# Attention by bit patterns: two shifted copies summed by an accumulating DMA, two value passes a tile for three

## The chip, the cores and the metric

The kernel runs on one core of a Trainium2 chip. The metric is device time in microseconds (us): the median of three runs is 708.62 us (708.62 to 708.87). One more execution was recorded by the hardware profiler; its span, from the first to the last instruction, is 706.9 us. Engines are named as the profile names them: PE (TensorE) does matmuls, PEld its weight loads, DVE (VectorE) and ACT (ScalarE) read its results from PSUM, POOL (GpSimd) works on SBUF only, and SP (SyncE) issues DMAs. L1280 is line 1280 of the kernel before.

## The reference

```python
def reference(A_x, A_wq, A_wk, A_wv, A_wo, B_x, B_w1, B_w2):
    # S = 2048 rows, D = 640, 32 query heads of 20, one shared key and value head, F = 1728
    xn = layernorm(A_x)
    q = (xn @ A_wq) in 32 heads;  k = xn @ A_wk;  v = xn @ A_wv
    p = softmax(q k^T / sqrt(20))
    return A_x + (p v) @ A_wo + silu(xn @ B_w1) @ B_w2
```

Most of the work is the attention's exponentials: 32 heads times 2048 queries times 2048 keys.

## The kernel before

**Tiles.** Keys are cut into 16 tiles of 128 (`kt`), queries into four chunks of 512, heads into eight sets of four; a group `g` is one query chunk with one set of heads, 32 groups in all. An item is one head, one group and one key tile: a score matrix of 128 keys x 512 queries, which fills one of the eight PSUM banks. There are 32 x 16 x 4 = 2048 items. PE makes the scores of an item with one matmul (`s_mm`, L1005); the four heads of a set use four different 32-row parts of the array, so up to four such matmuls run side by side. The products with the values are collected over all 16 key tiles in bank 7 (`UB`): one *value pass* (`pv_mms`, L1125) is four matmuls of 512 columns, one for each head.

**Two ways to an exponential.** ACT computes it exactly, two or three items at a time (L1090), and its tile then needs one value pass. DVE makes an approximation instead: L1280 (`p1`) adds a bias to the scores, which come in units of 1/128 of a power of two, and writes them as 16-bit integers; those bits, read as bf16, are a crude exponential whose error repeats with the fraction. Four items (all heads of one `g`, `kt`) form a *batch* in a buffer `z` of 128 x 2048. Two more copies with the bits shifted by 43 and by 85 (`SHIFT`) are then made from it: the first by DVE (L1321, buffer `s1`), the second by POOL (L1316, buffer `s2`; `POOL_J`). The three copies are weighted by `C_J` and averaged, which removes most of the error. The weights are put into three scaled copies of the values (`v_all`), and the sum of the three is made by three value passes into bank 7.

**Buffers.** There are three buffers for `z`, and two more once the query weights in them have been used; two each for `s1` and `s2` (`NW`), and a third for each once the query and hidden-layer jobs have read a part of the normalized input (`xnT`). A `z` is free again when all value passes of its batch are done, an `s1` or `s2` when the pass that reads it is.

**Other work.** PE also makes the query projections (q), the hidden layer of the feed-forward part (h) and the outputs (out, y, fin), all with `col_mm` (L395). At the end of a group DVE copies bank 7 away (L1173), and the division by the softmax sum goes through a reciprocal (L780), small DMAs on SP (L777, L782, L785), a multiply on POOL (L789) and DMAs to the place where the output matmuls read (L802).

**What sets the order.** The program holds a list scheduler (`Sched` and the loop at the end of `build`). It models each engine with written-out costs and builds one fixed instruction list for each engine: at each step the engine that is earliest in the model takes its best ready operation. Engines run their lists in order and wait for each other by semaphores (`emit`); when something comes later on the chip than in the model, the order does not change. PE takes ACT's next scores first; scores for DVE are taken when a bank is free and DVE would run dry (`dve_items`), and key tiles that DVE does not claim (`claim`) go to ACT. So the share of DVE follows from the model. `PLAN` is a string with one letter for every 10 us of modelled time; each letter picks a small variation of the rules. Operations marked `port` (L1316, L1321, L789) are kept from overlapping between DVE and POOL in the model, and `calm` makes L1316 and L789 wait for the last L1321 placed before them.

The profiled execution has 157 batches, that is 628 items on DVE and 1420 on ACT, and 3304 matmuls in value passes: 1420 and 157 x 12.

Of the kernel before, what the change touches and what calls it, by code (L numbers as in the profile page):

```python
# [8 lines left out]
BF16 = mybir.dt.bfloat16  # L9
# [17 lines left out]
LOG2E = math.log2(math.e)  # L27
QSCALE = 128.0 * LOG2E / math.sqrt(DH)
ESCALE = math.log(2.0) / 128.0
SHIFT = (0, 43, 85)  # L30
C_J = (1.0, 0.78515625, 0.62109375)
C_K = 0.32331863
ZBIAS = 128.0 * 127.0 + 128.0 * math.log2(C_K)
NJ = len(SHIFT)

ABUFS = ((0, 1, 2), (3, 4))
UB = 7
# [29 lines left out]
LOOKP = 1.0  # L67
POOL_SHIFT = 1900.0
POOL_J = (2,)
SWITCH = 105.0  # L70
SPRIO = 0.5
PIECE = 10000.0
# [18 lines left out]
RULES = dict(a={}, b=dict(keep=0.0), c=dict(lagp=3), d=dict(lagp=5), e=dict(lagp=0), f=dict(patience=200.0), g=dict(dwant=0.0),  # L91
             h=dict(zcap=4), i=dict(zcap=3), j=dict(homes=0), k=dict(leadmax=-1.0, lead=-1.0), l=dict(lead=0.08, leadmax=0.1),
             m=dict(need=560.0), n=dict(hold=0.0), o=dict(stay=460.0), p=dict(open=1), q=dict(slack=400.0), r=dict(hungry=1000.0), s=dict(claim=9), t=dict(open=3), u=dict(claim=4), v=dict(want=2))
PLAN = "baauqaocarjonimairnmrfnfdqmoomfujapcnmocdndifrjnaajoadarpmnrodqaqqnmada"


def rule(n):
# [45 lines left out]
def t_act(n):  # L143
    return 50.0 + 0.8333 * n
# [135 lines left out]
def build(nc, A_x, A_wq, A_wk, A_wv, A_wo, B_x, B_w1, B_w2, out, stack):  # L280
# [31 lines left out]
    wo_sb = sb([P, DC, D], BF16)  # L312
    wv_sb = sb([P, DC, SLOT], BF16)
    kT_rep = sb([P, S], BF16)
    v_all = sb([P, NJ, KT, SLOT], BF16)
    qT = sb([P, NQ, QW], BF16)
    Ebuf = sb([P, NSLOT * QW], BF16)
    z_t = [sb([P, HG * QW], BF16) for _ in range(NZ)]
# [121 lines left out]
    def zeros(n, k=QW):  # L440
# [1 line left out]
        return bass.AP(zero_t, z.offset, [list(z.ap[0]), [0, n], [1, k]])  # L442

    vw = v_all[:, :, :, :].rearrange("p j t r -> p (j t r)").rearrange("p (n k) -> p n k", k=QW)
    vms = act(lambda a: a.activation(vw, zeros(NJ * KT * SLOT // QW), AF.Copy), t_act(NJ * KT * SLOT), pre=[zero_op],
              reads=[res("zero")], writes=[res("v")], prio=0.6)
    v1s = []
    for j, cj in enumerate(C_J):
# [696 lines left out]
    def pv_reg(op, g, flags):  # L1145
        def com(op):
            flags["first"] = not pv_started[g]
            pv_started[g] = True
            pv_left[g] -= 1
            att["value"] += 1.0 if op.name.startswith("PV" + str(g)) else 1.0 / NJ  # L1150
            flags["last"] = pv_left[g] == 0
            if pv_left[g] == 0:
                end_group(g, op)
        op.on_commit = com
        op.gate = lambda: att["pgroup"] == g
        pv_ops[g].append(op)
# [58 lines left out]
    def claim():  # L1215
        if z_slot() is None:
            return None
        g = att["sgroup"]
        left = len(unclaimed[g]) if g < NGR else 0
        if left < ru.claim and g < NGR - 1:  # L1220
            g += 1
        if g >= NGR or len(unclaimed[g]) == 0 or g not in q_op or not all(o.done for o in q_op[g]):
            return None
        if len(unclaimed[g]) < (ru.claim if g < NGR - 1 else max(ru.claim, 9)):
            return None
        ready = [kt for kt in unclaimed[g] if kt in kT_op and kT_op[kt].done and all(o.done for o in v_op[kt // 4])]
        if not ready:
            return None
        kt = ready[-1]
        unclaimed[g].remove(kt)  # L1230
        pv_left[g] += NJ - 1
        return (g, kt)

    ln_done = [False]
# [53 lines left out]
    def dve_advance(job):  # L1288
        st = job.batch
        st["left"].remove(job.head)  # L1290
        st["p1"].append(job.consumers[0])
        if st["left"]:
            return
        open_b.remove(st)
        g, kt, zi = st["g"], st["kt"], st["zi"]
        z = z_t[zi]
        zr = [res("z", zi, i) for i in range(HG)]
        N = HG * QW
        closed.append(st)
        z16 = z[:, :].bitcast(I16)  # L1300
        st["nth"] = len(closed)
        src = [([z[:, i * QW:(i + 1) * QW] for i in range(HG)], st["p1"], zr)]
        for j in range(1, NJ):
            qk = XQ[j - 1]
            if qk is not None and len(s_last[j - 1]) == NW[j - 1] and len(xq_read[qk]) == DC + FC and all(o.done for o in xq_read[qk]):
                s_last[j - 1].append(sc.order["pe"][-1])
            wi = min(range(len(s_last[j - 1])), key=lambda k: -1 if s_last[j - 1][k] is None or k == NW[j - 1] and isinstance(s_last[j - 1][k], Op) else s_last[j - 1][k]["nth"])
            old = s_last[j - 1][wi]
            s_last[j - 1][wi] = st
            lent = wi == NW[j - 1]  # L1310
            t = xnT[:, 0:HG, qk * QW:(qk + 1) * QW] if lent else s_t[j - 1][wi][:, :]
            zin = z16.rearrange("p (h q) -> p h q", h=HG) if lent else z16
            r = res("s", j, wi)
            args = dict(pre=st["p1"] + ([idb] + [norm_op[n] for n in range(NT)] if old is None else [old] if isinstance(old, Op) else [old["pv"][j]]), reads=zr, writes=[r], name=f"s{j}")
            if j in POOL_J:
                op = pool(lambda v, t=t, j=j, zin=zin: v.tensor_scalar(t.bitcast(I16), zin, float(SHIFT[j]), 1.0, ALU.add, ALU.mult),  # L1316
                          POOL_SHIFT, prio=0.3, **args)
                op.port = True
                op.gate = calm(op)
            else:  # L1320
                op = dve(lambda v, t=t, j=j, zin=zin: v.tensor_scalar_add(t.bitcast(I16), zin, float(SHIFT[j])), t_dve(N, 4),  # L1321
                         prio=SPRIO - 0.01 * j, **args)
                op.port = True
                op.on_commit = shifts.append
            src.append(([t[:, i, :] if lent else t[:, i * QW:(i + 1) * QW] for i in range(HG)], [op], [r]))
        st["sh"] = [pre[0] for _, pre, _ in src[1:]]
        st["pv"] = []
        for j, (t, pre, rd) in enumerate(src):
            flags = {}

            def f(pe, t=t, j=j, flags=flags):
                lst = [(v_all[:, j, kt, :], t[i], i) for i in range(HG)]
                return pv_mms(pe, g, lst, flags["first"], flags["last"])
            pv = Op("pe", f, 222.0, pre=pre + v_op[kt // 4], reads=rd + [res("vv", kt // 4, j)],
                    writes=[sc.banks[UB]], mode="p", prio=1.5, name=f"PVd{g}_{kt}")
            pv_reg(pv, g, flags)
            st["pv"].append(pv)
# [438 lines left out]
def emit(nc, sc, dma_sems, sem):  # L1776
# [8 lines left out]
    for e, ops in order.items():  # L1785
        for op in ops:
            for d in op.deps:
                if d.eng == "sp":
                    continue
                if d.eng == e and e == "pe":  # L1790
                    continue
                needed.add(d)
# [19 lines left out]
    while n_done < total:  # L1812
        moved = False
        for e in order:
            while ptr[e] < len(order[e]):
                op = order[e][ptr[e]]
                if any(d not in clock for d in op.deps if not (d.eng == e)):
                    break
                know = last[e]
                req = {}  # L1820
                for d in op.deps:
                    if d.eng == "sp":
                        k, v = ("d", d.dma_sem), dval[d]
                    else:
                        if d.eng == e and e == "pe":
                            continue
                        k, v = ("e", d.eng), val[d]
                    if know.get(k, 0) < v:
                        req.setdefault(k, (0, None))
                        if v > req[k][0]:  # L1830
                            req[k] = (v, d)
                items = sorted(req.items(), key=lambda kv: -kv[1][1].seq)
                for k, (v, d) in items:
                    if know.get(k, 0) >= v:
                        continue
                    s = dma_sems[k[1]][0] if k[0] == "d" else esem[k[1]]
                    prog[e].append(("w", s, v))
                    know[k] = v
                    for kk, vv in clock[d].items():
                        if know.get(kk, 0) < vv:  # L1840
                            know[kk] = vv
                if op.dma_sem is not None:
                    prog[e].append(("d", op.fn, dma_sems[op.dma_sem][0]))
                elif op in needed:
                    prog[e].append(("i", op.fn, esem[e]))
                else:
# [86 lines left out]
```

## Time and profile before

| what | value |
|---|---|
| median of three runs | 708.62 us |
| span of the profiled execution | 706.9 us |
| granted TensorE clock, mean | 0.999 |
| ACT: first exponentials to the end, busy | 100 to 680 us: 577.1 of 580 us |
| DVE busy, 50 to 680 us | 565.9 of 630 us |
| POOL busy, 100 to 680 us | 304.2 of 580 us |
| DMA engines' mean share, 100 to 680 us | 0.22 to 0.26 in windows of 100 us (0.25 in the last, of 80 us) |
| bytes moved by DMA in the span | 28.97 MB |

The rows are from the page's head and from a table of busy time by windows. An engine's busy time counts what its instructions took, without overlaps; the time of one instruction can overlap the next one's, so a mean times a count can exceed it. A PE that is busy is not a PE at its peak, since its matmuls are pipelined. "Idle before, releaser" is the time an engine stood still before a group of instructions, and what ended it.

### The profile page before, as it was taken

How to read it: one execution, taken by the hardware profiler on the slowest of the kernel's cores; microseconds unless marked ns; L12 is line 12 of the kernel's file. 1: busy time of each engine (PE TensorE's matmuls, PEld its weight loads, DVE VectorE, ACT ScalarE, POOL GpSimd, SP SyncE). 2: the span in 40 equal slices, each digit the busy share in tenths (PEclk: the TensorE clock that was granted, in tenths of full speed). 3: DMA queues.
4: the chain of work that ended last, by engine and by line, in shares of the span. 5: the costliest groups of instructions: out<-in, count | busy, mean ns of one | idle time of the engine just before them, and what ended most of it. 6: DMA issues, size and time to landing. Idle time of an engine off the chain costs nothing.

```text
span 706.9 us, 22620 instructions
## 1 busy us (share of the span) xinstructions
PE 687.3 (97%) x9900; PEld 232.5 (33%) x9903; DVE 614.8 (87%) x1057; ACT 687.4 (97%) x730; POOL 360.2 (51%) x233
## 2 busy tenths in 40 slices
PE   8999999999999999999999999999999999999997
PEld 5432222222223333322233333322222233333334
DVE  7789999998999978899988889899889998887972
ACT  6999999999999999999999999999999999999994
POOL 6625645555456545555445455455554656544441
PEclk9999999999999999999999999999999999999999
DMA  8642221122221122322012222222222022232201
GB/s 220 199 144 39 19 21 18 32 31 30 18 30 17 22 39 29 67 34 26 16 21 29 29 38 33 55 30 27 29 20 21 7 32 32 32 63 29 18 7 39
DMA packets 34242, 28.97 MB, mean 41 GB/s; under 512 B 15487, under 2 KB 29663, under 8 KB 34143
## 3 DMA queue, kind: packets, MB, share of 16 engines
q1 hardware_dynamic: 33854, 27.20, 24.9%
q8 instruction: 77, 1.26, 0.7%
q10 hardware_dynamic: 288, 0.33, 0.1%
q14 instruction: 23, 0.18, 0.1%
HBM read 11.09 MB, written 2.62 MB: 19 GB/s over the span
## 4 chain that ended last, share of the span: by engine, by line
ACT 59%; PE 36%; DVE 2%; DMA 1%; POOL 0%; issue 0%; SPq 0%; DVEq 0%; POOLq 0%
ACT sbt L1090 56%; PE psall L1005 12%; PE psall L395 11%; PE psall L1125 11%; ACT sbt L709 3%; DMA sbt<-in_A_x_dram 1%; DVE sbt L1280 1%; PE psall L558 0%; DMA sbt<-in_A_wk_dram 0%; PE psall L532 0%; DVE sbt L894 0%; PE psall L1586 0%; PE psall L926 0%; PE psall L944 0%; DVE sbt L544 0%
## 5 line engine op out<-in xcount | busy, mean ns | idle before, releaser
L1090 ACT ACTIVATE sbt<-psall 128x1024 bf16<-128x1024 f32 (+1 forms) x658 | 666.1, 1227 | 4.5 <-PE psall L1005 3.9
L1280 DVE TENSOR_SCALAR sbt<-psall 128x512 int16<-128x512 f32 x628 | 412.5, 685 | 56.8 <-PE psall L1005 51.8
L1316 POOL TENSOR_SCALAR sbt<-sbt 128x2048 int16<-128x2048 int16 x157 | 298.2, 1899 | 303.3 <-DVE sbt L1321 112.0
L1005 PE MATMUL psall<-sbt 32*128 32x512 bf16 x2048 | 268.6, 384 | 9.0 <-ACT sbt L1090 5.4
L1125 PE MATMUL psall<-sbt 128*32 128x512 bf16 x3304 | 261.7, 384 | 2.7 <-DVE sbt L1173 2.5
L395 PE MATMUL psall<-sbt 128*32 128x320 bf16 (+2 forms) x3904 | 231.8, 331 | 0.6 <-DVE sbt L1280 0.2
L1005 PEld LDWEIGHTS psall<-sbt 32*128 32x128 bf16 x2048 | 71.4, 91 | 252.5 <-ACT sbt L1090 181.2
L395 PEld LDWEIGHTS psall<-sbt 128*32 128x32 bf16 x3904 | 83.8, 95 | 84.0 <-issue 53.0
L1321 DVE TENSOR_SCALAR sbt<-sbt 128x2048 int16<-128x2048 int16 x157 | 109.6, 709 | 1.8
L1125 PEld LDWEIGHTS psall<-sbt 128*32 128x32 bf16 x3304 | 65.5, 94 | 115.8 <-issue 76.8
L789 POOL TENSOR_TENSOR sbt<-sbt 128x512 bf16<-128x512 f32 x30 | 38.3, 1275 | 17.5 <-DVE sbt L1321 13.5
L712 DVE SCALAR_TENSOR_TENSOR sbt<-sbt,psall 128x512 bf16<-128x512 bf16 x52 | 35.4, 681 | 5.0 <-ACT sbt L709 2.9
L709 ACT ACTIVATE sbt<-psall 128x512 bf16<-128x512 f32 x52 | 39.3, 755 | 0.0
L1173 DVE COPY sbt<-psall 128x512 f32<-128x512 f32 x31 | 21.2, 683 | 0.1
L1586 PE MATMUL psall<-sbt 128*32 128x256 bf16 (+1 forms) x312 | 19.3, 355 | 1.2 <-DVE sbt L424 1.2
L630 DVE TENSOR_SCALAR sbt<-psall 128x512 bf16<-128x512 f32 x20 | 13.7, 683 | 0.5 <-PE psall L395 0.3
L831 DVE SCALAR_TENSOR_TENSOR sbt<-psall,sbt 128x320 bf16<-128x320 f32 x24 | 11.6, 483 | 1.7 <-PE psall L395 1.5
L522 POOL TENSOR_SCALAR sbt<-sbt 128x640 bf16<-128x640 bf16 x12 | 10.5, 880 | 2.3 <-DVE sbt L514 2.2
L1586 PEld LDWEIGHTS psall<-sbt 128*32 128x32 bf16 x312 | 8.8, 112 | 6.7 <-issue 2.3
L509 POOL TENSOR_TENSOR sbt<-sbt 128x2 f32<-128x2 f32 x8 | 5.6, 695 | 6.3 <-DVE sbt L507 6.2
L500 DVE BATCH_NORM_STATS2 sbt<-sbt 128x6 f32<-128x320 bf16 x14 | 6.5, 473 | 2.1 <-DMA sbt<-in_A_x_dram 1.9
L846 DVE SCALAR_TENSOR_TENSOR sbt<-psall,sbt 128x320 f32<-128x320 f32 x8 | 3.9, 482 | 4.8 <-PE psall L395 4.8
(61 smaller groups left out, 98.8 us busy)
## 6 DMA issues: line engine op xcount, KB each, us to landing
sbt<-sbt SPq DMA_DIRECT2D x120, 64.0 KB, 3.8
sbt<-in_A_x_dram SPq DMA_DIRECT2D x28, 160.0 KB, 4.1
sbt<-sbt SPq DMA_DIRECT2D x213, 20.0 KB
out_dram<-sbt SPq DMA_DIRECT2D x14, 160.0 KB, 1.9
sbt<-in_B_w_dram SPq DMA_DIRECT2D x1, 2160.0 KB, 11.4
sbt<-in_B_w_dram SPq DMA_DIRECT2D x1, 2080.0 KB, 8.1
sbt<-sbt SPq DMA_DIRECT2D x75, 8.0 KB
sbt<-in_A_wq_dram SPq DMA_DIRECT2D x1, 800.0 KB, 7.5
```

The lines of the kernel that those rows point to most:

```text
L395: ins = pe.matmul(ps[j * SLOT:(j + 1) * SLOT, b * BANK + off:b * BANK + off + n], w[:, j * SLOT:(j + 1) * SLOT], x, start=start, stop=stop ...
L709: t = Op("act", lambda a: a.activation(t_buf[0:rows, ts, :], bk(job.bank, 0, QW, rows=rows), AF.Tanh, scale=0.5), t_act(512), 215, pre=[jo ...
L712: u = Op("dve", lambda v: v.scalar_tensor_tensor(out=hT[par][0:rows, fk, :], in0=t_buf[0:rows, ts, :], scalar=1.0, in1=bk(job.bank, 0, QW, ...
L789: nm = pool(lambda e: e.tensor_tensor(oU[:, us, :], U_sb[:, us, :], Rrep, ALU.mult), 1350.0 + MARGIN, pre=[uc] + lc + pack_op.get(divmod(g ...
L1005: return pe.matmul(bk(b), kT_rep[i * SLOT:(i + 1) * SLOT, kt * P:(kt + 1) * P], qT[i * SLOT:(i + 1) * SLOT, g % NQ, :], start=True, stop=T ...
L1090: return a.activation(Ebuf[:, es * QW:es * QW + w], ps[:, buf[0] * BANK:buf[0] * BANK + w], AF.Exp, scale=ESCALE)
L1125: ins = pe.matmul(ps[i * SLOT:(i + 1) * SLOT, UB * BANK:UB * BANK + QW], lhsT, rhs, start=(first and k < HG), stop=(last and k >= len(lst) ...
L1173: uc = Op("dve", lambda v: v.tensor_copy(U_sb[:, us, :], bk(UB)), t_dve(512), 140, pre=[pv] + up, reads=[sc.banks[UB]], writes=[res("U", u ...
L1280: p1 = Op("dve", lambda v: v.tensor_scalar(z16[:, i * QW:(i + 1) * QW], bk(job.bank), ZBIAS, 0.0, ALU.add, ALU.max), t_dve(QW), 140, pre=[ ...
L1316: op = pool(lambda v, t=t, j=j, zin=zin: v.tensor_scalar(t.bitcast(I16), zin, float(SHIFT[j]), 1.0, ALU.add, ALU.mult), POOL_SHIFT, prio=0 ...
L1321: op = dve(lambda v, t=t, j=j, zin=zin: v.tensor_scalar_add(t.bitcast(I16), zin, float(SHIFT[j])), t_dve(N, 4), prio=SPRIO - 0.01 * j, **args)
L1586: ins = pe.matmul(ps[i * SLOT:(i + 1) * SLOT, UB * BANK:UB * BANK + n], zero_t[:, 0:SLOT], zero_t[:, 0:n], start=fresh, stop=fresh, tile_p ...
```

## The change

There are three shifts as before, now 0, 41 and 81, and the two shifted copies get the same weight. They can then be added before PE sees them: once L1321 and L1316 have written `s1` and `s2` of a batch, POOL issues one DMA that adds `s2` (128 x 2048 bf16, 512 KB) onto `s1` in place. A batch has two value passes, of `z` and of the sum; `v_all` keeps two scaled copies of the values. `s2` is free when the sum has landed, `s1` when the second pass is done. The model charges the DMA 1.0 us on POOL and 4.0 us more until it has landed, and treats it as a `port` operation. All engines' orders are computed anew with the new costs, and `PLAN` is another string.

```diff
-SHIFT = (0, 43, 85)
-C_J = (1.0, 0.78515625, 0.62109375)
-C_K = 0.32331863
+SHIFT = (0, 41, 81)
+C_J = (1.0, 0.65625)
+C_K = 0.3387
 NJ = len(SHIFT)
+NV = len(C_J)
...
+SUM_OCC = 1000.0
+SUM_LAT = 4000.0
...
-PLAN = "baauqaocarjonimairnmrfnfdqmoomfujapcnmocdndifrjnaajoadarpmnrodqaqqnmada"
+PLAN = "aaaqarpjrqaaprnpkrmmfhtqroaandodrmaaqaqmaadmrmtpqopmhtrqtnnqakrapankt"
...
-    v_all = sb([P, NJ, KT, SLOT], BF16)
+    v_all = sb([P, NV, KT, SLOT], BF16)
...
-        pv_left[g] += NJ - 1
+        pv_left[g] += NV - 1
...
+        held = []
...
-            args = dict(pre=st["p1"] + (... else [old["pv"][j]]), reads=zr, writes=[r], name=f"s{j}")
+            args = dict(pre=st["p1"] + (... else [old["sum"]] if j == 2 else [old["pv"][1]]), reads=zr, writes=[r], name=f"s{j}")
...
+            held.append(t if lent else t.rearrange("p (h q) -> p h q", h=HG))
...
+        (t1, p1, r1), (_, p2, r2) = src[1:]
+        tot = dma(f"sum{s1_home}", lambda e, a=held[0], b=held[1]: e.dma_start(a, b, accum_op=ALU.add), 0, pre=p1 + p2, reads=r2, writes=r1, prio=0.25, eng="pool")
+        tot.occ, tot.lat, tot.port = SUM_OCC, SUM_LAT, True
+        st["sum"] = tot
         st["pv"] = []
-        for j, (t, pre, rd) in enumerate(src):
+        for j, (t, pre, rd) in enumerate((src[0], (t1, [tot], r1))):
...
-                if d.eng == "sp":
+                if d.dma_sem is not None:
```

More of the change, by code (lines that the diff above doesn't have):

```diff
@@ L444, in build @@
     vw = v_all[:, :, :, :].rearrange("p j t r -> p (j t r)").rearrange("p (n k) -> p n k", k=QW)
-    vms = act(lambda a: a.activation(vw, zeros(NJ * KT * SLOT // QW), AF.Copy), t_act(NJ * KT * SLOT), pre=[zero_op],
+    vms = act(lambda a: a.activation(vw, zeros(NV * KT * SLOT // QW), AF.Copy), t_act(NV * KT * SLOT), pre=[zero_op],
               reads=[res("zero")], writes=[res("v")], prio=0.6)
@@ L1149, in com @@
             pv_left[g] -= 1
-            att["value"] += 1.0 if op.name.startswith("PV" + str(g)) else 1.0 / NJ
+            att["value"] += 1.0 if op.name.startswith("PV" + str(g)) else 1.0 / NV
             flags["last"] = pv_left[g] == 0
@@ L1310, in dve_advance @@
             lent = wi == NW[j - 1]
+            s1_home = wi if j == 1 else s1_home
             t = xnT[:, 0:HG, qk * QW:(qk + 1) * QW] if lent else s_t[j - 1][wi][:, :]
@@ L1313, in dve_advance @@
             r = res("s", j, wi)
-            args = dict(pre=st["p1"] + ([idb] + [norm_op[n] for n in range(NT)] if old is None else [old] if isinstance(old, Op) else [old["pv"][j]]), reads=zr, writes=[r], name=f"s{j}")
+            args = dict(pre=st["p1"] + ([idb] + [norm_op[n] for n in range(NT)] if old is None else [old] if isinstance(old, Op) else [old["sum"]] if j == 2 else [old["pv"][1]]), reads=zr, writes=[r], name=f"s{j}")
             if j in POOL_J:
@@ L1821, in emit @@
                 for d in op.deps:
-                    if d.eng == "sp":
+                    if d.dma_sem is not None:
                         k, v = ("d", d.dma_sem), dval[d]
```

## The prediction

> **What bounds the kernel now.** I read the page's busy times first, then the chain that ended last, then the groups of instructions with their releasers, then DVE's busy time by windows.
>
> ```profile
> PE 687.3 (97%) x9900; PEld 232.5 (33%) x9903; DVE 614.8 (87%) x1057; ACT 687.4 (97%) x730; POOL 360.2 (51%) x233
> ...
> ACT 59%; PE 36%; DVE 2%; DMA 1%; POOL 0%; issue 0%; SPq 0%; DVEq 0%; POOLq 0%
> ```
>
> ACT and PE are both full, and the chain goes back and forth between them: there is no single bound. DVE has 92 us free, POOL half its time.
>
> ```profile
> L1090 ACT ACTIVATE sbt<-psall 128x1024 bf16<-128x1024 f32 (+1 forms) x658 | 666.1, 1227 | 4.5 <-PE psall L1005 3.9
> L1280 DVE TENSOR_SCALAR sbt<-psall 128x512 int16<-128x512 f32 x628 | 412.5, 685 | 56.8 <-PE psall L1005 51.8
> L1316 POOL TENSOR_SCALAR sbt<-sbt 128x2048 int16<-128x2048 int16 x157 | 298.2, 1899 | 303.3 <-DVE sbt L1321 112.0
> ...
> L1125 PE MATMUL psall<-sbt 128*32 128x512 bf16 x3304 | 261.7, 384 | 2.7 <-DVE sbt L1173 2.5
> ...
> L1321 DVE TENSOR_SCALAR sbt<-sbt 128x2048 int16<-128x2048 int16 x157 | 109.6, 709 | 1.8
> ```
>
> ACT is never short of scores (4.5 us idle before 658 exponentials). DVE is: 51.8 us of its idle time ends with a score matmul. So PE time saved helps ACT only by a detour: PE feeds DVE earlier, DVE claims more batches, and ACT has fewer items.
>
> ```profile
> 300.79 0.39 PE L395 MATMUL psall<-sbt 128*32 128x512 bf16 x4
> 301.12 0.45 PE L1005 MATMUL psall<-sbt 32*128 32x512 bf16 x3
> 301.50 0.61 PE L395 MATMUL psall<-sbt 128*32 128x512 bf16 x8
> 302.05 0.39 PE L1005 MATMUL psall<-sbt 32*128 32x512 bf16 x2
> 302.37 0.61 PE L395 MATMUL psall<-sbt 128*32 128x512 bf16 x8
> ```
>
> Four matmuls show 0.39 us and eight 0.61, so one more pass of four costs PE 0.22 us. From one score set to the next is 0.93 us, filled without a gap.
>
> ```profile
> 100.00:150.00 50.00, 47.26 (x78) 1.00 0.28 31
> ...
> 400.00:450.00 50.00, 42.00 (x67) 1.00 0.22 30
> 450.00:500.00 50.00, 47.55 (x80) 1.00 0.26 39
> ```
>
> These windows (length, DVE busy, instructions, clock, DMA share, GB/s) show where room is: 42.0 of 50 us where PE makes output matmuls, 47.6 elsewhere. From 50 to 680 us DVE is idle 630 - 565.9 = 64 us.
>
> **The change, part by part.**
>
> *The third pass goes.* 157 x 0.22 = 34.5 us of PE time. By itself that shortens nothing, as ACT stays full.
>
> *Batches move from ACT to DVE.* An item costs ACT 666.1/1420 = 0.469 us, a batch 1.88 us. A batch costs DVE 4 x 412.5/628 + 109.6/157 = 3.33 us. If n batches move, the span falls by 1.88n, and DVE's idle time falls by (3.33 + 1.88)n = 5.2n. What idle time is left? In its fullest window before DVE has 2.4 of 50 us idle (47.6 busy), which would be 30 us in 630 and n = 6.5; none left would be n = 12.3. The waits on scores occur in the full windows too, so I take half of 30: (64 - 15)/5.2 = 9.4 batches, 17.7 us. From both sides: 12 us (n = 6.5) to 23 us (n = 12.3). PE then has about 687 - 34.5 + 2 = 655 us of work in 689, and its cover is real: were PE still full, n would be 0.
>
> *POOL's new issue.* No DMA is issued by POOL before. The bounds are 0.1 us (its smallest memset row) and 1.9 us (its own pass over the same tile); SP's issues of copies inside SBUF take 0.59 us median (L785). I take 1.0, between the near row and the upper one. 166 x 1.0 on POOL's 360 gives about 535 of 689 us: not a bound, so nothing in the sum; at 1.9 it would be 690, full. The issue waits for L1321 and for POOL's own L1316; behind it in POOL's list stand the next L1316 and the multiply L789, and behind L789 SP waits at L802 (103.6 us already, in SP's own waits), with the query copies of L643 behind that. POOL's 303 us of idle time before L1316 hides this.
>
> *The sum's way.* Before, the last pass followed L1316; now it follows L1316, the issue and the landing. Landing times by row:
>
> ```profile
> sbt<-sbt SPq DMA_DIRECT2D x120, 64.0 KB, 3.8
> ...
> out_dram<-sbt SPq DMA_DIRECT2D x14, 160.0 KB, 1.9
> sbt<-in_B_w_dram SPq DMA_DIRECT2D x1, 2160.0 KB, 11.4
> sbt<-in_B_w_dram SPq DMA_DIRECT2D x1, 2080.0 KB, 8.1
> ...
> sbt<-in_B_w_dram SPq DMA_DIRECT2D x2, 80.0 KB, 2.3
> ```
>
> The bounds are 1.9 us (a third of the bytes) and 11.4 (four times). Between 80 KB at 2.3 and 2080 KB at 8.1 lie 2.9 us per 1000 KB. An addition must read both tiles, 1024 KB: 2.3 + 2.7 = 5.0 us. Started from the 64 KB row, a copy inside SBUF but out of a single row per head, it is 6.6. I take 5.0. The order allows 1.0 + 4.0 = 5.0, so PE has no wait in the sum; each microsecond beyond is priced with the rivals.
>
> The page "DMA: Bandwidth & Descriptors" of the Trainium skill (section "Anatomy of one DMA — SWDGE (gpsimd) path") fits 2.0 us plus the bytes at 436 GB/s for DMAs from GpSimd; as an estimate that is 3.2 us for 512 KB and 4.4 us with both tiles counted. By it the sum stays as it is, and the late landing below would be worth a chance of only 0.1.
>
> *Buffers.* `s1` is now held for 0.7 + 1.9 + 5.0 and some 2 us until PE gets to it, 9.6 us. A batch comes every 630/150 or so = 4.2 us: three buffers (12.6 us) suffice, two (8.4 us) do not, until the third is lent. I charge nothing: `z` and the later two thirds of the run are free of it, and until then it can cost at most one batch in eight, some 3 batches or 6 us; I keep that for the range.
>
> *Small things.* Four value scalings less on DVE (L590, 2.2/12 each) are 0.7 us of DVE, 0.3 us of span. Weights, shifts and the smaller `v_all` cost nothing: no instruction is added for them.
>
> **The sum.** 706.9 - 17.7 - 0.3 = 688.9 us of span; the runs' median lies 1.7 above the span before, so I add 1.7 and get 691 us.
>
> **The rivals.**
>
> *The sum lands late (slower).* Place: the second value pass in PE's fixed list. For it: 64 KB inside SBUF already take 3.8 us, and a row of one size scatters (11.4 and 8.1 for nearly the same bytes); DMA engines that stand at 0.2 now will carry some 87 MB more. Against it: L1316's passes hardly ever held PE before (2.1 us in nine waits, in the waits list), so the list leaves room. Price: from a batch's last score to its second pass is about 10 us, so a lateness of d is paid about 630/10 = 63 times, not once a batch, since PE's wait also delays what follows. The point from which it decides is 18/63 = 0.3 us beyond the room left. With 6.6 us instead of 5.0 and 1 us of room: 63 x 0.6 = 38 us, 691 + 38 = 729 us; without room 691 + 101 = 792.
>
> *The DMA engines fill up (slower).* The busiest window moves 277 GB/s at a share of 0.82. At that rate of 338 GB/s when full, 512 KB take 1.6 us and three times that (two reads, a write) 4.7; times 166 is 257 to 772 us, beside about 0.24 x 689 = 165. Only at the upper end does it bind: 772 + 165 = 937 us. From 3.2 us a sum on, it decides.
>
> *POOL and DVE block each other (a smaller gain).* One L1321 at 409.67 us took 2.03 us instead of 0.69 and ended just after three back-to-back L1316 passes: while POOL is at SBUF, this pass waits. A 1.0 us issue overlaps a 0.7 us L1321 at random with chance 1.7/4.2 = 0.4 and costs some 0.5 us then: 166 x 0.2 = 33 us of DVE, 33/5.2 x 1.88 = 12 us of span: 703 us. Against it: the order keeps the two apart, and only a few of 157 were longer than 0.9 us.
>
> The page "SBUF — State Buffer" of the Trainium skill (section "SBUF: two separate sides") speaks against this change: while VectorE runs in a two-port mode, GpSimd cannot write the descriptors of its DMAs, and the transfer stands still. The trace shows the block in the other direction only (the 2.03 us). By that rule a sum would be up to 0.7 us later, which belongs to the first rival.
>
> *The relief is not used (no change).* DVE's windows at 47.6 of 50 are nearly full, and the new order may give it no more batches; then ACT stays at 666 us and the time at 708.
>
> **How the numbers follow.** Forecast 691: 0.58, with its own range 681 to 700 (the bounds 12 and 23 us around it, and the buffers). Smaller gain, 703: 0.10. No change, 708: 0.06. Late sum, 729: 0.23. Full DMA engines: 0.03. Below 0.2%, 1.4 us, no change can be told from the measurement. Faster: 0.58 + 0.10 + 0.01 = 0.69; same 0.04; slower 0.23 + 0.03 + 0.01 = 0.27. The range goes from 679 to 729: the upper half of the late case and the full engines are left out, 0.15, and a little below.
>
> **What would show it.** Right: L1125 falls from 3304 to about 2700 matmuls, L1280 rises to about 665, ACT's L1090 falls to about 650 us and stays without idle time, DVE's idle before L1280 falls below 25 us, sums land within 5 us. Wrong: PE's weight loads for value passes wait for a DMA for more than a few us in all (late sum); L1321 means above 0.8 us (blocking); POOL above 90% busy; the DMA share near 1; L1280 still near 628 (relief not used).

## The result, and the profile after

The changed kernel takes 888.28 us (median of four runs, 883.88 to 891.53) against 708.75 us before (708.62 to 708.91): 1.253 times the time, 95% interval 1.2506 to 1.2553. The prediction was 691 us. The profiled execution has a span of 884.8 us, 177.9 us more than before. In the new listing the lines stand three lower in the first part and a few more behind the new code: L1093 is ACT's exponential, L1283 `p1`, L1321 POOL's shift, L1326 DVE's shift, L1334 the sum, L1128 the value pass, L1008 the scores, L792 the multiply of the normalization, L783 its reciprocal, L788 its last small DMAs.

From the page of the changed kernel: busy times, the clock granted to PE and the DMA engines' busy share in 40 slices (tenths), the DMA queues (packets, MB, share of 16 engines), the chain that ended last.

```profile
PE 745.4 (84%) x9704; PEld 236.0 (27%) x9707; DVE 632.8 (72%) x1048; ACT 705.2 (80%) x742; POOL 518.3 (59%) x387
...
PEclk9998998788889989999989798999788998799999
DMA  8676776767776868778569776777857777796773
...
q0 software_dynamic: 40128, 81.80, 53.4%
q1 hardware_dynamic: 33854, 27.20, 18.9%
...
DMA 34%; PE 23%; DVE 17%; POOL 12%; issue 8%; ACT 4%; SPq 3%; POOLq 0%; DVEq 0%
```

ACT and PE have fallen from 97% to 80% and 84%. The chain, 59% ACT before, is 34% DMA, and 33 of these points are transfers inside SBUF. The sums alone keep the sixteen DMA engines busy for 53.4% of the span; the clock, 0.999 in the mean before, is 0.906.

The groups of instructions (count, busy us, mean ns, idle before and what ended most of it):

```profile
L1093 ACT ACTIVATE sbt<-psall 128x1024 bf16<-128x1024 f32 (+1 forms) x670 | 676.8, 1111 | 156.3 <-PE psall L1008 154.3
L1283 DVE TENSOR_SCALAR sbt<-psall 128x512 int16<-128x512 f32 x624 | 410.0, 684 | 162.9 <-PE psall L1008 159.7
...
L1128 PE MATMUL psall<-sbt 128*32 128x512 bf16 x2672 | 243.8, 416 | 109.3 <-DMA sbt<-sbt 103.5
...
L1334 POOL DMA_DIRECT2D sbt<-sbt x156 | 162.1, 1084 | 131.6 <-DVE sbt L1326 104.8
L1326 DVE TENSOR_SCALAR sbt<-sbt 128x2048 int16<-128x2048 int16 x156 | 128.4, 837 | 7.7 <-PE psall L1128 7.2
...
L792 POOL TENSOR_TENSOR sbt<-sbt 128x512 bf16<-128x512 f32 x30 | 40.5, 1348 | 73.7 <-DMA sbt<-sbt 42.1
```

ACT's exponentials grew by 10.7 us and their idle time by 151.8 (4.5 before): together 162.5 of the 177.9. That idle time ends with a score matmul, so PE was late; and PE stood 103.5 us ahead of value passes for a DMA. DVE's items are 624, not more than the 628 before.

The DMA issues (count, KB, median us from issue to landing):

```profile
sbt<-sbt POOLq DMA_DIRECT2D x156, 512.0 KB, 6.4
sbt<-sbt SPq DMA_DIRECT2D x120, 64.0 KB, 5.4
```

The sum lands after 6.4 us (4.5 at least, 12.1 at most), where the order was made for 5.0. The small DMAs of the normalization, which the change does not touch, take 5.4 us in place of 3.8, and up to 9.7 (4.8 before). Part of that is their issue on SP, 1.08 us in the median for 0.59. Behind them stand POOL's L792 (42.1 us of waits in 12 places; 2.7 before) and DVE's L783 (19.3; none before). Behind the sums stand PE's value passes (the 103.5 us, in 58 places) and POOL's L1321, which may not write an `s2` that a sum still reads (35.3 us in 21 places). Followed back through the trace by the instruction that issued each transfer, the chain that ended last holds 248 us of sums in 31 pieces and 47 us of the normalization's small DMAs in nine.

One stall in PE's timeline (start us, us, instructions; in brackets the wait ahead of them):

```profile
399.93 0.40 PE L398 MATMUL psall<-sbt 128*32 128x512 bf16 x4
402.36 0.40 PE L1128 MATMUL psall<-sbt 128*32 128x512 bf16 x4 [2.04 <-DMA sbt<-sbt]
402.59 0.39 PE L398 MATMUL psall<-sbt 128*32 128x512 bf16 x4
403.73 0.40 PE L1128 MATMUL psall<-sbt 128*32 128x512 bf16 x4 [0.75 <-DVE sbt L1176]
...
404.88 1.90 PE L1128 MATMUL psall<-sbt 128*32 128x512 bf16 x16
```

And the busy times around it (stretch, its length, busy us of each engine with counts, clock, DMA share, GB/s):

```profile
400.00:404.00 4.00, 1.22 (x16) 0.25 (x16) 4.00 (x4) 2.31 (x3) 3.77 (x3) 1.00 0.48 92
404.00:406.00 2.00, 2.00 (x22) 0.66 (x22) 1.56 (x3) 1.43 (x2) 1.72 (x2) 0.56 0.87 126
406.00:408.00 2.00, 2.00 (x24) 0.57 (x16) 0.00 (x0) 0.93 (x2) 1.05 (x1) 0.59 1.18 172
```

PE waits 2.04 us for a sum and 0.75 us for the copy of bank 7, which stood on DVE behind two shifts that took 4.04 us together. Then its clock is 0.56 to 0.59 for 4 us: sixteen matmuls take 1.90 us, 0.43 a pass by their weight loads where a pass took 0.22. So this wait is paid again just after it. Over the run the missing clock is at most (1 - 0.906) x 884.8 = 83 us. PE is busy for 745.4 us; the same list of 9704 matmuls keeps it busy for 684.8 us at a clock of 1.0 (e2 below), 61 us less. How much of this lies on the path is not measured.

### The profile page after: what moved, and what is told of

Its sections match the earlier page's. It is cut to its first block, busy times and chain, and to the rows that moved or that the text cites. A ratio compares the mean times of both kernels' runs of the same rounds, so it can differ in the third digit from the quotient of the medians.

```text
span 884.8 us, 22460 instructions
## 1 busy us (share of the span) xinstructions
PE 745.4 (84%) x9704; PEld 236.0 (27%) x9707; DVE 632.8 (72%) x1048; ACT 705.2 (80%) x742; POOL 518.3 (59%) x387
## 3 DMA queue, kind: packets, MB, share of 16 engines
q0 software_dynamic: 40128, 81.80, 53.4%
## 4 chain that ended last, share of the span: by engine, by line
DMA 34%; PE 23%; DVE 17%; POOL 12%; issue 8%; ACT 4%; SPq 3%; POOLq 0%; DVEq 0%
DMA sbt<-sbt 33%; POOL sbt L1321 8%; PE psall L1008 8%; DVE sbt L1283 8%; PE psall L1128 7%; PE psall L398 7%; DVE sbt L1326 4%; ACT sbt L1093 4%; POOL sbt L1334 2%; PE psall L1596 1%; DVE sbt L1176 1%; SPq L805 1%; POOL sbt L792 1%; DVE sbt L715 1%; SPq L788 1%
## 5 line engine op out<-in xcount | busy, mean ns | idle before, releaser
L1093 ACT ACTIVATE sbt<-psall 128x1024 bf16<-128x1024 f32 (+1 forms) x670 | 676.8, 1111 | 156.3 <-PE psall L1008 154.3
L1283 DVE TENSOR_SCALAR sbt<-psall 128x512 int16<-128x512 f32 x624 | 410.0, 684 | 162.9 <-PE psall L1008 159.7
L1321 POOL TENSOR_SCALAR sbt<-sbt 128x2048 int16<-128x2048 int16 x156 | 295.2, 1892 | 133.4 <-DVE sbt L1326 52.4
L1128 PE MATMUL psall<-sbt 128*32 128x512 bf16 x2672 | 243.8, 416 | 109.3 <-DMA sbt<-sbt 103.5
L1008 PE MATMUL psall<-sbt 32*128 32x512 bf16 x2048 | 297.5, 414 | 14.9 <-DVE sbt L1283 9.2
L398 PE MATMUL psall<-sbt 128*32 128x320 bf16 (+3 forms) x3904 | 259.2, 356 | 6.7 <-DMA sbt<-sbt 4.1
L1334 POOL DMA_DIRECT2D sbt<-sbt x156 | 162.1, 1084 | 131.6 <-DVE sbt L1326 104.8
L1008 PEld LDWEIGHTS psall<-sbt 32*128 32x128 bf16 x2048 | 72.9, 92 | 277.2 <-ACT sbt L1093 120.5
L1326 DVE TENSOR_SCALAR sbt<-sbt 128x2048 int16<-128x2048 int16 x156 | 128.4, 837 | 7.7 <-PE psall L1128 7.2
L1128 PEld LDWEIGHTS psall<-sbt 128*32 128x32 bf16 x2672 | 57.5, 97 | 228.0 <-DMA sbt<-sbt 125.9
L398 PEld LDWEIGHTS psall<-sbt 128*32 128x32 bf16 x3904 | 87.0, 98 | 105.3 <-issue 68.4
L792 POOL TENSOR_TENSOR sbt<-sbt 128x512 bf16<-128x512 f32 x30 | 40.5, 1348 | 73.7 <-DMA sbt<-sbt 42.1
L1596 PE MATMUL psall<-sbt 128*32 128x256 bf16 (+1 forms) x748 | 53.2, 364 | 1.2 <-DVE sbt L427 1.2
L715 DVE SCALAR_TENSOR_TENSOR sbt<-sbt,psall 128x512 bf16<-128x512 bf16 x52 | 35.3, 678 | 3.8 <-ACT sbt L712 2.3
L712 ACT ACTIVATE sbt<-psall 128x512 bf16<-128x512 f32 x52 | 33.2, 638 | 1.3 <-PE psall L398 1.3
L1596 PEld LDWEIGHTS psall<-sbt 128*32 128x32 bf16 x748 | 18.9, 104 | 21.5 <-issue 14.9
L783 DVE RECIPROCAL sbt<-sbt 128x16 f32<-128x16 f32 x30 | 7.4, 247 | 19.3 <-DMA sbt<-sbt 19.3
```

The costliest lines, as they stand in the source:

```text
L398: ins = pe.matmul(ps[j * SLOT:(j + 1) * SLOT, b * BANK + off:b * BANK + off + n], w[:, j * SLOT:(j + 1) * SLOT], x, start=start, stop=stop ...
L712: t = Op("act", lambda a: a.activation(t_buf[0:rows, ts, :], bk(job.bank, 0, QW, rows=rows), AF.Tanh, scale=0.5), t_act(512), 215, pre=[jo ...
L715: u = Op("dve", lambda v: v.scalar_tensor_tensor(out=hT[par][0:rows, fk, :], in0=t_buf[0:rows, ts, :], scalar=1.0, in1=bk(job.bank, 0, QW, ...
L792: nm = pool(lambda e: e.tensor_tensor(oU[:, us, :], U_sb[:, us, :], Rrep, ALU.mult), 1350.0 + MARGIN, pre=[uc] + lc + pack_op.get(divmod(g ...
L1008: return pe.matmul(bk(b), kT_rep[i * SLOT:(i + 1) * SLOT, kt * P:(kt + 1) * P], qT[i * SLOT:(i + 1) * SLOT, g % NQ, :], start=True, stop=T ...
L1093: return a.activation(Ebuf[:, es * QW:es * QW + w], ps[:, buf[0] * BANK:buf[0] * BANK + w], AF.Exp, scale=ESCALE)
```

## The experiments

The theories went by letters. L: the sum is late for its value pass. P: the issue on POOL and the blocking of DVE cost the time, whatever is moved. R: the relief of PE is worth nothing. G: a group claims its last batches too late for the sum. Q: the sums' load on the DMA engines delays other DMAs. W: the sum's way is so long that the three `s1` buffers bind. A ratio stands with its 95% interval; line numbers of the experiments' kernels differ by up to three. Diffs are against the changed kernel unless another is named.

**How much is moved.** Three kernels have the same order on every engine. The first adds a quarter (one head of four), the second replaces the DMA by a memset of one column on POOL, the third copies in place of adding.

```diff
-e.dma_start(a, b, accum_op=ALU.add)
+e.dma_start(a[:, 0:1, :], b[:, 0:1, :], accum_op=ALU.add)     # e1_quarter
+e.memset(nosum[:, n:n + 1], 0.0)                              # e2_stub
+e.dma_start(a, b)                                             # e3_copy
```

> The changed kernel with its order and all its waits, but each sum moves one head's 512 columns of the four (128 KB instead of 512 KB); three heads of the second pass stay without the s2 part. Theory L (the sum lands later than the fixed order allows: 6.4 us median, up to 12.1, against 1.0 + 4.0): landing falls to 3 to 4 us, PE's waits for it (103.5 us) fall below 15 us, the granted clock goes back to 0.99, the time to 710 to 730 us. Rival P (POOL's issue and its blocking with DVE cost it, L1326 128 us and 1.08 us an issue): the issue stays, so the time stays above 840 us.

> The changed kernel's order with a one-column memset on POOL in place of the sum: the addition is left out, the wait on POOL stays. Theory L: the same 710 to 730 us as with a quarter of the bytes, within 5 us of it. Rival P: far below the run with a quarter of the bytes (more than 50 us). Rival R (the third pass was never worth anything, since PE time was not what kept batches from DVE): not below 705 us, with L1283 at 624 instructions as the order is the same. My prediction's sum (17.7 us from moved batches) would have 691 us for an order without lateness.

> The changed kernel's order, with a plain copy of s2 over s1 by the same DMA in place of the addition (the addition is left out). If the reading of both tiles for the addition makes the sum late: landing at 4 us or less, time 720 to 760 us. If it is the 512 KB and the issue by POOL: landing stays at 5.5 us or more and the time above 840 us. L is for the first to the extent that the landing falls, and for a time that goes with the landing.

| kernel | time, us | ratio to before | sum lands, us | SP's small DMAs, us | PE waits for DMA at L1128, us |
|---|---|---|---|---|---|
| e2_stub | 716.47 | 1.0112 [1.0091, 1.0132] | none | 3.8 | none |
| e1_quarter | 727.67 | 1.027 [1.0242, 1.0297] | 3.1 | 4.2 | 9.0 |
| e3_copy | 745.31 (the other of two runs: 759.54) | no interval | 4.0 | 4.7 | 25.1 |
| the change | 888.28 | 1.253 [1.2506, 1.2553] | 6.4 | 5.4 | 103.5 |

The last three columns of e3 are from the run of 759.54 us. The new order by itself costs 8 us (spans 714.9 and 706.9); all the rest, 172 us, comes with the transfer, and steeply. P falls: in the quarter the issue takes 0.95 us (1.08 in the change) and L1326 736 ns (837), and it is 11 us above the stub. That distance was a miss, since I expected the two within 5 us; the quarter's time, its waits and its clock (0.992) are those that L expected. The copy came out as L expected. With a median of 4.0 us it lands within the 5.0 that the order allows, but 55 of its 156 landings are later, up to 7.6 us, and it is 29 us above the stub.

The stub's groups also show what became of PE's time (L1094 is the exponential, L1597 a *filler*: matmuls of zeros that the scheduler puts where PE has nothing else, meant to keep its clock up):

```profile
L1094 ACT ACTIVATE sbt<-psall 128x1024 bf16<-128x1024 f32 (+1 forms) x670 | 667.8, 1230 | 5.6 <-PE psall L1009 4.6
...
L1597 PE MATMUL psall<-sbt 128*32 128x256 bf16 (+1 forms) x748 | 49.5, 343 | 1.2 <-DVE sbt L428 1.2
```

The fillers before, on that profile's page:

```profile
L1586 PE MATMUL psall<-sbt 128*32 128x256 bf16 (+1 forms) x312 | 19.3, 355 | 1.2 <-DVE sbt L424 1.2
```

Fillers take 49.5 us (748 matmuls); before they took 19.3 (312). Of the 34.5 us that the third pass frees, 30 are filled with zeros, and ACT has as much to do as before.

**Two passes without a sum.** `s2` is written but not read, so that the second pass takes `s1` alone; nothing is moved. All orders are computed anew. The second of these kernels has other letters of `PLAN`, chosen for it, in 13 places (its expectation says ten).

```diff
-        tot = dma(f"sum{s1_home}", ...)
-        for j, (t, pre, rd) in enumerate((src[0], (t1, [tot], r1))):
+        for j, (t, pre, rd) in enumerate((src[0], (t1, p1, r1))):
```

> The sum is left out altogether: two value passes, z and s1, s2 is still written by POOL but not read, and all orders are computed anew without any cost for a sum. This prices the first step of the prediction alone. My step (34.5 us of PE time bring 9.4 more batches to DVE): L1283 at 665, time 691 us. Rival R: L1283 within 20 of 628, time 703 to 712 us.

> The run with two passes and no sum at all (e4, 710 us; s2 is written but not read) with ten of PLAN's letters changed to suit an order without a sum. My step (34.5 us of PE time bring batches to DVE, 17.7 us) was only hidden by letters made for another order: at or below 695 us and L1283 near 665. Rival R (PE time is not what keeps batches from DVE): 698 to 706 us, L1283 within 25 of 628.

710.01 us, 1.0015 [1.0006, 1.0025], and 705.3 us, 0.995 [0.9933, 0.9966]. R holds in both. From the first one's groups:

```profile
L1283 DVE TENSOR_SCALAR sbt<-psall 128x512 int16<-128x512 f32 x640 | 415.5, 683 | 54.7 <-PE psall L1008 51.6
...
L1593 PE MATMUL psall<-sbt 128*32 128x256 bf16 (+1 forms) x524 | 36.3, 348 | 1.2 <-DVE sbt L427 1.2
```

PE has 34 us less to do, and DVE waits for scores as long as before: 51.6 us now, 51.8 then. It gets 640 items, three batches more; the new letters make it 644 and 39.1 us of waiting. So in these two orders the relief is worth between nothing and 3 us, not 17.7.

**An order that knows the landing.** If L in its narrow form were all, it would be enough to tell the scheduler the true landing time, 6.4 us. The first of the next three kernels, e5, does that. The other two do it with an empty `PLAN`; e7 claims batches earlier in a group (`claim` 10 for 6), and e8 is its control.

```diff
-SUM_LAT = 4000.0
+SUM_LAT = 6400.0          # e5_late_order; e7 and e8 too, with PLAN = ""
-BASE = dict(..., claim=6)
+BASE = dict(..., claim=10)   # e7_early_claim alone
```

> The changed kernel with one number altered: the order is computed for a sum that lands 6.4 us after its issue instead of 4.0 (SUM_LAT), the median that the trace showed. Theory L in its narrow form (the harm is only that the fixed order did not know of it): PE's waits for DMA fall from 103.5 to below 30 us and the time to 715 to 760 us. Rival W (the length of the way itself binds: a buffer s1 is held some 13 us, three buffers cannot feed a batch every 4.4 us, and nothing else is ready for PE): the time stays above 800 us, with fewer batches than 156 or with more filler matmuls than 748.

> The changed kernel with an order computed for a landing of 6.4 us, without the letters of PLAN, and with DVE allowed to claim a key tile only while ten of the group's sixteen are unclaimed (six before). Theory G (the end of a group: bank 7 is handed on only when the group's last sum has landed and been used, so a batch claimed late makes everything wait): 730 to 770 us, PE's waits for DMA below 30 us, fewer than 145 batches, and at least 60 us faster than its control with six. Rival W (three s1 buffers bind): within 20 us of the control.

> The control: the same landing of 6.4 us and no letters, claims down to six unclaimed tiles as in the changed kernel. Theories G and W both: 820 to 890 us.

The late order takes 881.06 us, 1.2432 [1.2396, 1.2468]; the early claim 836.58, 1.1808 [1.1717, 1.19]; the control 862.87, 1.218 [1.2105, 1.2254]. The late order takes PE's waits for DMA at L1128 from 103.5 to 40.6 us and brings 7 us: narrow L falls. In exchange POOL's L792 waits 68.2 us for DMAs (42.1 in the change). It has 145 batches and 1924 filler matmuls, the signs that W had named; but DVE's L1326 waits only 17.3 us for the passes that free an `s1`, so W is not shown. Leaving out the letters brings 18 us. Early claims bring 26 us more, where G had asked for 60 and W for less than 20: both miss, and G is a small part.

**The DMA by itself.** A small kernel of its own: 128 x 2048 bf16 tiles in SBUF, one DMA after the other.

> No attention at all: a measurement of the disputed DMAs on an idle chip, 128 x 2048 bf16 each, eight at a time: accumulating from GpSimd one after another; plain copy from GpSimd; plain copy from SP; two accumulating ones in flight; accumulating ones while DVE runs passes like L1326 without end. If the adding itself makes it slow: some 4.5 us (the shortest in the changed kernel) alone against some 3 us for the copy, and near 7 us for two in flight. If DVE's passes hold up the issue: the last group is at least 0.7 us longer than the first. If the 6.4 us come from other traffic alone, the first group is below 3.5 us.

The timeline of POOL (start us, duration of the issue us, wait ahead): L38 is the accumulating DMA, L41 the plain copy.

```profile
12.58 0.86 POOL L38 DMA_DIRECT2D a<-b  x1 [3.96 <-DMA a<-b]
17.35 0.86 POOL L38 DMA_DIRECT2D a<-b  x1 [3.90 <-DMA a<-b]
...
49.29 0.54 POOL L41 DMA_DIRECT2D a<-b  x1 [2.65 <-DMA a<-b]
52.42 0.53 POOL L41 DMA_DIRECT2D a<-b  x1 [2.59 <-DMA a<-b]
```

A lone sum takes 17.35 - 12.58 = 4.77 us with its issue, a copy 3.13. Two sums in flight take 7.7 us for the pair, one of them 6.6 to land. Under DVE passes without a pause a sum takes 5.12 us, 0.35 more, of which 0.30 are POOL's issue (1.16 us for 0.86). So 5.0 us was a good price for one sum with nothing beside it. In the kernel a sum's engine time is 0.534 x 884.8 / 156 = 3.03 us of all sixteen; a copy's (28.9% of 757.7 us, e3) is 1.40.

**Load without the sum.** This kernel is the one *before*, with its three passes and the same order on PE, DVE, ACT and SP. POOL issues in addition two plain copies of `s2` into unused DRAM for each L1316, each 512 KB; only the next writer of that `s2` waits for them (14.4 us in all). The last kernel of this part does the same with 16 columns in place of 2048: the same issues and almost no load.

```diff
+for k in range(2):
+    bg = dma(f"bg{wi}_{k}", lambda e, n=n, b=held: e.dma_start(spare[n]..., b), 0, pre=p2, reads=r2, eng="pool")
+    bg = ... e.dma_start(spare[n][:, 0:16], b[:, 0, 0:16])      # e11_issue_only
```

> The kernel before with its three value passes and the same order on PE, DVE, ACT and SP, plus the traffic alone: after each L1316 POOL issues two plain copies of s2 (512 KB each) to a spare place in DRAM, and no engine waits for them but POOL, before it writes that s2 buffer again. Two copies take the DMA engines about as long as one accumulating sum (2 x 1.4 against 2.7 to 3.0 us). Theory L (the wait in the value pass is the harm): 708 to 730 us. Rival Q (the traffic delays the small DMAs of the normalization, L789 waits for them at the head of POOL's list, and all behind it is late): L785 lands at 5 us or more instead of 3.8, L789 waits for DMA above 40 us, and the time is above 760 us.

> The traffic run again with the same POOL issues in the same places (two for each L1316, awaited by nobody but POOL), but each copies 16 columns of 128 x 2048 instead of all, so that POOL's issues and their blocking with DVE stay and the DMA engines' load goes. If the load on the DMA engines made the 840 us: 708 to 722 us, L785 lands at 4 us or less. If POOL's issues and the blocking of L1321 made it: above 790 us, the mean of L1321 stays near 0.93 us.

The added copies make 840.54 us, 1.1862 [1.1828, 1.1896]: 132 us more than before (the change: 180), without a sum, without a wait of a value pass for a DMA, in an order that was good for 708. All of Q's signs came. L, as the only way to such a loss, falls; for the changed kernel, whose PE does wait for sums, this run does not exclude it. Its queue and small DMAs on the page:

```profile
q0 software_dynamic: 45216, 164.65, 52.0%
...
sbt<-sbt SPq DMA_DIRECT2D x120, 64.0 KB, 5.4
```

and its waits (us in total, times, longest):

```profile
POOL sbt L792 <- DMA sbt<-sbt: 64.3, 17, 8.2
...
DVE sbt L783 <- DMA sbt<-sbt: 39.2, 12, 7.5
```

The load is that of the sums in time of the DMA engines (52.0 and 53.4%), though not in kind: these copies go to DRAM and move 164.65 MB, the sums 81.80. The small DMAs land as late as there, 5.4 us. POOL stands in its list behind L792 for 64.3 us, DVE behind L783 for 39.2 (2.7 and nothing before); then shifts come late and PE waits for POOL (27.7 us at L1128). The chain that ended last holds 100 us of small DMAs in 23 pieces and 25 us of the copies that POOL waits for. With 16 columns the time is 728.45 us, 1.0283 [1.0253, 1.0313], and the small DMAs land early again:

```profile
sbt<-sbt SPq DMA_DIRECT2D x120, 64.0 KB, 3.9
```

So 20 us are issues and blocking (DVE's shift takes 849 ns in the mean, 709 before), a little more than the 722 expected at most. The other 112 us come with the bytes; a part of them may be DVE's shift again, which takes 929 ns with the full copies.

**Moving the wait.** L792 goes to DVE, orders anew.

```diff
-nm = pool(lambda e: e.tensor_tensor(oU..., U_sb..., Rrep, ALU.mult), ...)
+nm = dve(lambda e: e.tensor_tensor(oU..., U_sb..., Rrep, ALU.mult), t_dve(QW), ...)
```

> The changed kernel with the normalization's multiply (L792) moved from POOL to DVE, all orders computed anew: sums no longer stand behind a multiply that waits for small DMAs. Some 18 us more work for DVE. Rival Q: the time falls below 830 us. Theory L without Q: 870 to 920 us, as the sums land as late as before (6 us or more) and DVE has more to do.

904.2 us, 1.276 [1.2702, 1.2819]. Q's expectation of less than 830 failed, and the time lies in the range of L without Q (870 to 920). DVE now waits 77.5 us for the same small DMAs ahead of L792, so the wait has moved from one in-order list to another, and this run does not tell the two theories apart.

**Telling the order of both.** As e7, with the sum taken as 8.0 us and SP's DMAs as 3.0 us later than in the model.

```diff
-SUM_LAT = 4000.0
+SUM_LAT = 8000.0
+SP_MORE = 3000.0
-            op.fin = self.dma_free + 700.0 + own
+            op.fin = self.dma_free + 700.0 + own + (SP_MORE if start > 50000.0 else 0.0)
```

> The run with the early claim (836.6 us) with two altered numbers: the order is computed for sums that land 8.0 us after the issue instead of 6.4, and for SP's DMAs that land 3.0 us later than before from 50 us on. If the harm is that the fixed lists stand in front of DMAs that come later than planned (sums and SP's small ones alike): 750 to 800 us, with the waits of PE and POOL for DMA less than half of 41 and 82 us and the granted clock above 0.97. If the load itself binds, planned or not: within 15 us of 836.

779.05 us, 1.0997 [1.0965, 1.1029], as expected: 57 us below e7 and 109 us below the change, though the transfers land as late as before (6.4 and 5.2 us). PE's waits for sums fall from 41.3 us in e7 to 3.9, POOL's at the multiply from 81.6 to 32.8. Both numbers were altered at once, so which of them brings how much is not shown. ACT's group:

```profile
L1094 ACT ACTIVATE sbt<-psall 128x1024 bf16<-128x1024 f32 (+1 forms) x686 | 709.2, 1247 | 28.3 <-PE psall L1009 27.6
```

The clock is back at 0.986. What stays is another cost: 132 batches in place of 157, so that ACT has 709.2 - 666.1 = 43 us more of exponentials, and 24 us more of idle time; together 67 of the 70 us.

**A version that beats both.** Two copies in place of three, shifts 0 and 64, the second by POOL: no sum, no DVE shift, two passes. The average is over two copies, and so coarser. Two thresholds of the order and `PLAN` were set for it.

```diff
-SHIFT = (0, 41, 81)
-C_J = (1.0, 0.65625)
+SHIFT = (0, 64)
+C_J = (1.0, 0.70703125)
-POOL_J = (2,)
+POOL_J = (1,)
-BASE = dict(..., slack=700.0, ..., stay=0.0, ...)
+BASE = dict(..., slack=300.0, ..., stay=460.0, ...)
```

> A kernel without DMA for the sum and with all its passes read: two shifts, 0 and 64, with weights 1 and 0.70703125, the second copy made by POOL alone, so that a batch costs DVE four L1283 and no L1326 and PE two passes; letters and two thresholds of the order suited to it. The approximation is coarser (one copy fewer in the average). It takes 110 us from DVE and 35 us from PE. If DVE and PE time is what binds: below 670 us. Rival R (score matmuls for DVE wait for PSUM banks that ACT's exponentials hold, so that neither counts in full): 686 to 696 us, with L1283 at 650 to 680 and DVE below 80% busy.

689.13 us, 0.9723 [0.9707, 0.9739]. L1091 is its exponential, L1281 its `p1`:

```profile
PE 669.0 (97%) x9623; PEld 222.9 (32%) x9623; DVE 548.4 (80%) x936; ACT 668.5 (97%) x725; POOL 377.5 (55%) x242
...
L1091 ACT ACTIVATE sbt<-psall 128x1024 bf16<-128x1024 f32 (+1 forms) x653 | 646.2, 1197 | 2.8 <-PE psall L1006 2.2
L1281 DVE TENSOR_SCALAR sbt<-psall 128x512 int16<-128x512 f32 x668 | 439.8, 686 | 102.5 <-PE psall L1006 98.3
```

Ten batches move to DVE and ACT's exponentials take 646.2 us, 20 less: a moved batch is worth 2.0 us, about what the prediction said (1.88). But it took 110 us of DVE time as well as PE's pass to move ten, and DVE then waits 98.3 us for scores. The numbers that rival R had named came (time, 668 items, DVE at 80%); that PSUM banks are the reason is not shown by them.

## Why the prediction was wrong, point by point

Two steps failed. The larger one is *The sum's way*, from which followed that "PE has no wait in the sum": PE waits 103.5 us for sums, and the same order without the transfer takes 716.47 us in place of 888.28 (e2). What the sums' load does to the small DMAs, and what holding `s2` does to POOL, had no term at all. The smaller one is *Batches move from ACT to DVE*: between nothing and 3 us came, not 17.7. Three of the prediction's own signs of being wrong are there: PE's weight loads for value passes wait 125.9 us for DMAs, DVE's shift takes 837 ns in the mean, and DVE has 624 items.

**What bounds the kernel: half right.** ACT is full and is helped only by a detour over DVE; in e14 that detour works at about the price given. But that PE is busy for 97% did not make it a bound: of the 34 us that a third of the batches' value passes took, it filled 17 (e4) to 30 (e2) with zeros, and ACT's work hardly fell.

**The third pass goes, PE has room: right.** L1128 has 2672 matmuls (about 2700 said).

**Batches move from ACT to DVE, 17.7 us: failed.** The premise was that DVE's idle time falls because PE, with less to do, feeds it earlier. "Ended by a score matmul" was read as "PE was too busy". With a third of the batches' value passes gone, DVE waits 51.6 us as before, PE spends half of the time on more fillers, and three or four batches move (e4, e13). The lower bound of 12 us was no bound; the rival "the relief is not used", at 0.06, had the right time for this part. What holds DVE's scores back instead is not shown. One candidate is PSUM banks that ACT still holds: in e4 PE's score loads wait 199.8 us for ACT's exponentials (181.2 before). But in e14, where DVE waits longest, it is 166.0 us. The scheduler's rule that feeds DVE only when it would run dry is the other candidate.

**POOL's issue, 1.0 us: right** (1.08; POOL 59% busy). "POOL's 303 us of idle hides this" was wrong all the same: idle time in the mean is no cover for a list that stands still behind L792, as L789 is now.

**The sum's way, 5.0 us: right for a lone sum, wrong here.** Alone 4.77, in the kernel 6.4 in the median and 12.1 at most. The rows of before come from DMA engines at 0.2 to 0.3; the price was for an empty road that this change itself fills. The 6.6 us that the prediction worked out and set aside lies near the 6.4 by luck, since a lone sum takes 4.77. The page "DMA: Bandwidth & Descriptors" of the Trainium skill (section "Anatomy of one DMA — SWDGE (gpsimd) path") gave an estimate of 3.2 us, which fits the lone copy's 3.13; for the adding DMA both its 3.2 and its 4.4 are too low, and the chance of 0.1 drawn from it was further off than my 0.23.

**The late sum, 729 us: right in its place, wrong in its price.** The median is 1.4 us over the 5.0; by the rival's own rule that is 63 x 0.4 = 25 us with its 1 us of room and 63 x 1.4 = 88 us without it, at most half of what came. The rule charged lateness by a median, at one place in PE's list. Missing was the term for every *other* DMA that a list stands behind: added copies alone, on the kernel before, cost 132 us, of which e11 leaves 20 to issues and blocking. A second part missing was the clock, which fell after the wait shown above: 0.906 in the mean, 0.986 once the order knows of the delays (e12).

**The DMA engines fill up: right in size, wrong as a threshold.** The sum's engine time is 3.03 us, within the 1.6 to 4.7, close to the 3.2 from which it was to bind. The engines are busy for 0.73 of the span, not full, and the damage is done: what counted is that transfers land later (sums after 6.4 us for 4.77 alone, small DMAs after 5.4 for 3.8), not whether the work fits into the span.

**Buffers: right for `s1`, not seen for `s2`.** DVE's L1326 waits only 7.2 us for the passes that free an `s1`. But an `s2` is held until its sum has landed, and POOL's L1321 waits 35.3 us for that.

**POOL and DVE block each other: happened.** L1326 takes 837 ns instead of 709: 156 x 0.13 = 20 us of DVE, beside 33 said. What that is worth where DVE is idle for 28% of the time is not measured. By the page "SBUF — State Buffer" (section "SBUF: two separate sides") of the Trainium skill the DMA would be the one that stands, if DVE's pass runs in a two-port mode, which no run here shows. Alone under DVE passes a sum was 0.35 us longer, 0.30 of it in POOL's issue, so that direction exists and is small here.

**Open.** Of the 180 us, 8 are the order and 172 come with the transfer (e2). How the 172 divide in the changed kernel itself is not measured: 11 to 20 (issues, blocking) and 112 (load) are from other kernels and need not add. Its own chain runs through sums for 248 us and through small DMAs for 47; e9 shows that the small DMAs' delay can be as dear without any sum, not that it is so here. A change that gives small DMAs a way past the sums was not tried, nor was the `s1` buffer's hold.

## What to carry to other kernels

Price a new transfer by its landing among the others like it, not alone, and by what its load does to every DMA that an in-order list already waits for; the engines need not be full. In a fixed order medians are not enough: in e9, small DMAs 1.6 us later in the median and with a tail to 9.7 us go with a loss of more than 100 us. Before relief of a full engine is counted, show that something is ready to use it: a stub with the work left out and the order made anew costs one run and tells it.

## What was not expected of the hardware

An adding DMA inside SBUF keeps the DMA engines busy 3.03 us for 512 KB, 2.2 times a copy's 1.40, and its issue on POOL takes 0.86 us alone against 0.53 (1.16 under DVE passes).

The clock fell to 0.56 after PE had been busy 1.22 of 4 us, with no single wait longer than 2.04 us. The page "TensorE: Matmul & The Clock Gate" of the Trainium skill (section "Part 1: The HAM clock gate (the "warmup" mystery)") puts the half clock after an idle window of about 3.4 us; here a window with some matmuls in it was enough.
